# Halo rows of the plain values copied on chip instead of loaded twice, and 29 scheduling offsets in place of 12

## The chip, the cores and the metric

The kernel runs on one core of a Trainium2 chip. A core has TensorE (PE: matmuls and transposes), VectorE (DVE), ScalarE (ACT), GpSimd (POOL) and SyncE (SP), each with its own queue of instructions in a fixed order, and 16 DMA engines that all queues share. The metric is device microseconds (us) of one execution; lower is better.

## The reference

Eight batches of attention over 576 tokens and 8 heads of 64 columns, followed by an MLP over all 4,608 tokens:

```python
mask_plain = (rel >= 0) & (rel < window)                              # window 32, heads 0 to 3
mask_dil = (rel >= 0) & (rel < window * dilation) & (rel % dilation == 0)   # dilation 4, heads 4 to 7
attn = softmax(where(mask, q @ k.T / 8, -1e9));  x = attn @ v        # x: [4608, 512]
h = x @ w_in                                                          # [512, 2048]
out = (h * sigmoid(beta * h)) @ w_out
```

A plain head looks back 31 tokens. A dilated head looks back at 32 tokens of its own residue class modulo 4.

## The kernel before

**Attention of a batch b.** Plain heads are cut into six blocks of 96 queries, each against 128 keys: its own 96 and the 32 ahead of them. So the plain values lie in SBUF in a tile vp of 128 rows per block: rows 32 to 127 hold the block's own 96 value rows, rows 0 to 31 (the halo, WIN = 32) the last 32 rows of the block before. There are two such tiles, for even and odd batches. Before the change, direct_vp (L414 to L421) fetches all 128 rows of each block from DRAM, so a quarter of the rows is fetched a second time; batch 0 has three loads (96 rows of the first two heads, their 32 halo rows, and the other two heads), every later batch one. Dilated heads work on 128 of the 144 tokens of each class (scores L659, values L764), and on the last 16 of each class together, the "tail" (scores T at L628, values U at L749). Queries and keys are needed with the 64 columns on the partitions: batches 0 to 2 load rows into staging tiles st and transpose them on TensorE (dilated L461, plain L468), with copies from PSUM into kT, qT, dk, dq; from these, VectorE or GpSimd make the tail's dkt (mixed, L555) and qt, in two halves (padded, L564). Batches 3 to 7 cast q and k into DRAM scratch on GpSimd's queue and transpose by DMA on SyncE's. Scores are followed by exp on ScalarE (L595) and, from batch 1 on, a multiplication by a 0/1 mask on VectorE or GpSimd (L599); values by a normalisation on VectorE (L614, L615); the result comes into xT through transposes on TensorE (batches 0 and 1) or through DRAM by DMA.

**MLP.** Nine token tiles t of 512 tokens: 16 slices fb of four matmuls each from xT (L863), tanh on ScalarE (L872), the gate into g on VectorE (L877), then four output blocks tb in four parts of four matmuls (L898) and an eviction by 0.5 (L913, L915).

**Order.** The work is written as some 1,300 operations, each with candidate engines and an estimated duration, dependencies, a due time vt and, for some, a PSUM bank group with a cap on how many may be held (CAPS). Plan.run, a list scheduler that runs when the program is built, places one operation after another on the engine where it can start first, and among operations that can start at about the same time it takes the one with the least vt. So the order of every queue is fixed at build time, and an engine waits for its next instruction even when a later one could run. NUDGE maps the number of an operation to an offset in ns that is added to its possible start when the operations are compared. The operations are numbered as they are created, so a new operation shifts the numbers behind it. Where TensorE would be free for over 300 ns early on, the scheduler puts a "filler" matmul on zeros (L1010).

**Loads.** GpSimd issues nearly all loads, in order. For each batch below 3 (loads, from L960): dilated k and q, plain k and q, dilated values vd16, two tail pieces vt, and vp. From batch 3 on a small copy, "pace" (L976), which waits for xT (or g) of two batches before, stands ahead of a batch's casts, vd, vt and vp. A copy "spread" moves dilated values from their landing place into vd. fill3 and fill4 set the column of ones behind the values and, in fill3, zero rows of vp.

Of the kernel before, what the change touches and what calls it, by code (L numbers as in the profile page):

```python
# [36 lines left out]
class Plan:  # L37
# [3 lines left out]

    CAPS = {"h": 3, "p": 4, "o": 2, "z": 4, "a": 8, "s": 5, "w": 6}
    SWITCH = 95
    NUDGE = {101: -60, 129: 400, 159: -400, 219: 60, 245: -150, 250: 900, 417: 900, 517: 60, 554: 900,
        700: -900, 789: 60, 1116: -900}
    LAT = {"PE": 210, "ACT": 45, "DVE": 45, "POOL": 60, "SP": 0}
    NEAR = {"PE": 40, "ACT": 60, "DVE": 60, "POOL": 60, "SP": 0}

# [131 lines left out]
def kernel(  # L180
# [10 lines left out]
    nc = tc.nc  # L191
    P = 128
    B, H, S, D = q.shape
# [5 lines left out]
    WIN = 32  # L199
# [8 lines left out]
    QT = 96  # L208
    NI = S // QT
# [5 lines left out]
    DIRECT = 3  # L215
# [14 lines left out]
    plan = Plan(range(8))  # L230
# [6 lines left out]
    def copy(e, out, in_):  # L237
        (nc.scalar.copy if e == "ACT" else E[e].tensor_copy)(out=out, in_=in_)  # L238
# [46 lines left out]
    vp = [const([P, 4 * NI, DV], BF16, f"vp{i}") for i in range(2)]  # L285
# [33 lines left out]

    def t_fill3(e):  # L320
        nc.vector.memset(vp[0][:, :, D:D + 1], 1.0)
        nc.vector.memset(vp[0][0:WIN, 0, 0:D], 0.0)
        nc.vector.memset(vd[0][:, :, :, D:D + 1], 1.0)
        nc.vector.memset(vt_[0][:, :, :, D:D + 1], 1.0)
    fill3 = plan.op([("DVE", 500)], t_fill3, vt=-7.8)
# [5 lines left out]
    fill4 = plan.op([("POOL", 800)], t_fill4, vt=-1.2)  # L331
# [58 lines left out]
    def load(queue, args, deps, vt, kb, rate=.4, issue=750, lat=1100):  # L390
        return plan.op(
            [(queue, issue)],
            lambda e: dma(queue, *args), deps, vt, dma=kb * 1024 / rate / 1000, lat=lat)
# [13 lines left out]
        return [plan.op([("ACT", 175 + .834 * RD * D), ("DVE", 160 + 1.042 * RD * D)],  # L407
                        lambda e, x=x: copy(e, std[0][:, x], stage[:, x]), [o], -9.1, sbuf=True) for x in range(2)]

    def plain_v(b, p0, c0):  # L410
        return bass.AP(tensor=v.tensor, offset=v[b, 0].offset + (p0 - WIN) * D + c0 * QT * D,
                       ap=[[D, P - WIN if p0 else WIN if c0 == 1 else P], [QT * D, 4 * NI - c0], [1, D]])

    def direct_vp(b, deps, vt):  # L414
        if b:
            return [load("POOL", (vp[b % 2][:, :, 0:D], plain_v(b, 0, 0)), deps, vt, 768, .27, 1450,
                         1100 if b < DIRECT else 4000)]
        half = 2 * NI
        return [load("POOL", (vp[0][WIN:P, 0:half, 0:D], plain_v(0, WIN, 0)[:, 0:half]), deps, vt, 288, .25),
                load("POOL", (vp[0][0:WIN, 1:half, 0:D], plain_v(0, 0, 1)[:, 0:half - 1]), deps, vt, 92, .25),  # L420
                load("POOL", (vp[0][:, half:, 0:D], plain_v(0, 0, half)), deps, vt, 384, .27)]  # L421

    def direct_vd(b, deps, vt, tdeps=()):
        src = v[b, 4:8].rearrange("h (t T) d -> t h (T d)", T=C)[0:P]
# [99 lines left out]
    def attention(b, ld, names, vts):  # L524
# [3 lines left out]
        kv = b % 2  # L528
        if b < DIRECT:
            for n in [x for x in names if x[0] in "KQ"]:  # L530
                z, kind, i = "KQ".index(n[0]), n[1], int(n[2])
                vt = vt_of[n]
# [22 lines left out]
        def mixed(e):  # L555
            copy(e, dkt[kv], dk[kv][:, :, :, CT - KTL:].rearrange("p r h k -> p h k r"))
        o = plan.op([("DVE", 450), ("POOL", 550)], mixed,
                    (steps["KD0"] + steps["KD1"] if b < DIRECT else ready["D"][0:1]) + war(("dkt", kv)), vt_of["T"] - .01, sbuf=True)
# [4 lines left out]
        for c in range(2):  # L563
            def padded(e, c=c):  # L564
# [3 lines left out]
            o = plan.op([("DVE", 250), ("POOL", 500)], padded,  # L568
                        (steps["QD0"] + steps["QD1"] if b < DIRECT else ready["D"][1:]) + [fill1] + war(("qt", kv)),
                        vt_of["T"] - .01, sbuf=True)  # L570
# [5 lines left out]

        vdeps = {}
        vt = vt_of["zVAL"]
        vdeps["P", 1] = [ld["vp"][-1], (fill3, fill4)[kv]]
        vdeps["P", 0] = (ld["vp"][:-1] or ld["vp"]) + [(fill3, fill4)[kv]]  # L580
        def spread(e):
            copy(e, vd[kv][:, :, :, 0:D], vd16_of[b])
        o = plan.op([("POOL", 1100), ("DVE", 620)], spread,
                    [ld["vd"][0], (fill3, fill4)[kv]] + war(("vd", kv)), vt, sbuf=True)
# [35 lines left out]
        for name in [n for n in names if n[0] in "ST"]:  # L620
            vt = vt_of[name]
# [370 lines left out]
    for t in range(NTT):  # L992
# [4 lines left out]
        b = t + 1  # L997
# [46 lines left out]
```

## Time and profile before

| | |
|---|---|
| times of three runs | 304.8, 304.99, 305.12 us; median 304.99 |
| the profiled execution | 304.8 us; its span, first to last instruction, 303.1 us |
| PE busy | 291.2 us, 96% of the span |
| DVE, ACT, POOL busy | 188.5 (62%), 169.6 (56%), 85.6 (28%) |
| granted TensorE clock | 0.999 |
| DMA | 42.76 MB, 117,377 packets; 63.8% of the 16 engines' time on GpSimd's queue, 37.3% on SyncE's |
| issue of a vp load on GpSimd | 10 of them, 1,798 ns on average |
| landing of a vp load | 6.2 to 18.9 us after issue |

How to read it: the page gives busy time by engine, then 40 slices of the span. A busy PE is not a PE at its peak, since matmuls overlap and their ends are modelled; a matmul of 512 columns is listed with some 379 ns, but on the chain of waits four of them take 0.86 us. The chain of waits goes back from the last instruction, at each step to what released it. It is PE for 86% of the span. Idle time of an engine that nothing waits for costs nothing. Some few per cent of matmul records are missing; a gap of 0.05 us after a group of three matmuls instead of four is one of those, no stop.

By the slices the DMA engines are at 0.9 or more busy from 8 us to about 205 us, and at 0.3 or less after about 215 us; GpSimd is idle from then on.

### The profile page before, as it was taken

Reading aid. Unit: us, or ns where it says so; the run is one execution under the profiler, and the core shown is the slowest. Engines: PE = TensorE matmul, PEld = TensorE weight load, DVE = VectorE, ACT = ScalarE, POOL = GpSimd, SP = SyncE. Lnnn points to the kernel's source line nnn. Section 1 sums busy time; section 2 is a strip of 40 time slices with the busy share of each in tenths; the row PEclk is TensorE's granted clock in tenths of the full one; section 3 lists DMA queues with packets and bytes.
Section 4 is the critical chain, followed back from the end, with each engine's and each line's share of the span. In section 5 each row is a group of like instructions: output and inputs, shape, how many; then the busy total and the mean of one; then the engine's idle time right before and its main releaser. Section 6 shows DMA issues by size and latency. Waiting matters only on the chain.

```text
span 303.1 us, 5956 instructions
## 1 busy us (share of the span) xinstructions
PE 291.2 (96%) x2268; PEld 149.0 (49%) x2306; DVE 188.5 (62%) x420; ACT 169.6 (56%) x304; POOL 85.6 (28%) x123
## 2 busy tenths in 40 slices
PE   8898899899999999999999999999999999999995
PEld 5655455454544545444544444544444444444454
DVE  4768976988955966695586556956852544343300
ACT  3767764776646663765574547555743544554411
POOL 8997322853028205520560073200000000000000
PEclk9999999999999999999999999999999999999999
DMA  7999999999879998999899979995033100010122
GB/s 160 181 210 200 207 179 211 172 167 139 216 153 174 157 206 165 192 145 224 165 180 169 224 139 153 169 190 150 37 93 93 38 35 36 35 37 35 51 87 71
DMA packets 117377, 42.76 MB, mean 141 GB/s; under 512 B 93749, under 2 KB 110725, under 8 KB 117349
## 3 DMA queue, kind: packets, MB, share of 16 engines
q0 software_dynamic: 66464, 19.37, 63.8%
q1 hardware_dynamic: 50740, 22.95, 37.3%
q8 instruction: 18, 0.29, 0.4%
q14 instruction: 11, 0.08, 0.1%
q10 hardware_dynamic: 144, 0.07, 0.1%
HBM read 39.32 MB, written 18.87 MB: 192 GB/s over the span
## 4 chain that ended last, share of the span: by engine, by line
PE 86%; DMA 4%; DVE 4%; issue 3%; POOL 1%; ACT 1%; POOLq 0%; DVEq 0%
PE bank L898 41%; PE bank L863 37%; DMA st<-in_k_dram 4%; PE bank L780 2%; PE bank L659 1%; PE bank L764 1%; DVE qt L238 1%; PE bank L687 1%; PE bank L461 1%; DVE dkt L238 1%; PE bank L749 1%; PE bank L723 1%; DVE dk L238 1%; DVE g L877 0%; POOL st L388 0%
## 5 line engine op out<-in xcount | busy, mean ns | idle before, releaser
L877 DVE SCALAR_TENSOR_TENSOR g<-tnh,bank 128x512 bf16<-128x512 bf16 x144 | 97.4, 684 | 67.9 <-ACT tnh L872 66.7
L872 ACT ACTIVATE tnh<-bank,beta_half 128x512 bf16<-128x512 f32 x144 | 98.3, 690 | 73.4 <-PE bank L863 70.4
L898 PE MATMUL bank<-w_out_bf,g 128*128 128x512 bf16 (+2 forms) x589 | 137.7, 367 | 1.6 <-issue 1.1
L863 PE MATMUL bank<-xT,w_in_bf 128*128 128x512 bf16 (+1 forms) x565 | 137.2, 376 | 1.1
L863 PEld LDWEIGHTS <-w_in_bf 128*128 128x128 bf16 x584 | 55.2, 98 | 61.5 <-issue 0.4
L898 PEld LDWEIGHTS <-g 128*128 128x128 bf16 x608 | 54.7, 98 | 56.5
L913 ACT ACTIVATE osb<-bank 128x512 f32<-128x512 f32 (+1 forms) x35 | 20.6, 589 | 33.3 <-PE bank L898 32.8
L595 ACT ACTIVATE pt<-bank 128x384 bf16<-128x384 f32 (+1 forms) x54 | 20.4, 470 | 7.2 <-PE bank L687 5.3
L595 ACT ACTIVATE ptd<-bank 128x512 bf16<-128x512 f32 x32 | 16.8, 603 | 6.2 <-PE bank L659 6.2
L599 DVE TENSOR_TENSOR pt<-pt,mask_n 128x384 bf16<-128x384 bf16 (+1 forms) x43 | 15.5, 376 | 6.5 <-ACT pt L595 6.1
L615 DVE TENSOR_TENSOR xsp<-bank,rcp 96x384 bf16<-96x384 f32 x32 | 17.7, 553 | 1.1
L388 POOL DMA_DIRECT2D vp<-in_v_dram x10 | 18.0, 1798 | 0.6 <-PE bank L802 0.6
L599 DVE TENSOR_TENSOR ptd<-ptd,mask_d 128x512 bf16<-128x512 bf16 x28 | 12.2, 448 | 5.4 <-ACT ptd L595 4.5
L614 DVE RECIPROCAL rcp<-bank 128x4 f32<-128x4 f32 (+2 forms) x72 | 12.9, 179 | 4.0 <-PE bank L764 2.2
L976 POOL COPY pace<-xT 1x2 bf16<-1x2 bf16 x4 | 0.7, 176 | 50.7 <-DMA xT<-x 50.7
L615 DVE TENSOR_TENSOR xdm<-bank,rcp 128x256 bf16<-128x256 f32 x32 | 13.6, 425 | 1.1
L388 POOL DMA_DIRECT2D vt<-in_v_dram x16 | 14.2, 1030 | 0.0
L388 POOL DMA_DIRECT2D s<-in_q_dram x10 | 13.7, 1369 | 0.0
L780 PEld LDWEIGHTS <-pt 128*128 128x128 bf16 x192 | 9.1, 97 | 5.1
L388 POOL DMA_DIRECT2D s<-in_k_dram x10 | 11.2, 1122 | 1.0 <-issue 0.9
L915 DVE TENSOR_SCALAR osb<-bank 128x512 f32<-128x512 f32 (+2 forms) x3 | 1.4, 469 | 14.6 <-PE bank L898 14.6
L780 PE MATMUL bank<-vp,pt 128*128 128x65 bf16 x192 | 9.9, 193 | 0.0
(106 smaller groups left out, 172.5 us busy)
## 6 DMA issues: line engine op xcount, KB each, us to landing
out_dram<-osb SPq DMA_DIRECT2D x35, 256.0 KB, 2.8
s<-in_k_dram POOLq DMA_DIRECT2D x10, 288.0 KB, 6.3
s<-in_q_dram POOLq DMA_DIRECT2D x10, 288.0 KB, 8.5
vp<-in_v_dram POOLq DMA_DIRECT2D x7, 384.0 KB, 18.1
w_out_bf<-in_moe_w_out_dram POOLq DMA_DIRECT2D x2, 1024.0 KB, 15.2
st<-in_q_dram POOLq DMA_DIRECT2D x6, 288.0 KB, 10.8
x<-xsp SPq DMA_DIRECT2D x12, 144.0 KB
st<-in_k_dram POOLq DMA_DIRECT2D x5, 288.0 KB, 13.3
```

The lines of the kernel that those rows point to most:

```text
L238: (nc.scalar.copy if e == "ACT" else E[e].tensor_copy)(out=out, in_=in_)
L388: {"POOL": nc.gpsimd, "SP": nc.sync}[queue].dma_start(out=out, in_=in_)
L595: nc.scalar.activation(out=w(), in_=sc(), func=ACT.Exp, scale=SCALE)
L599: E[e].tensor_tensor(out=w(), in0=w(), in1=m(), op=ALU.mult)
L614: nc.vector.reciprocal(out=r, in_=p[..., D])
L615: nc.vector.tensor_tensor(out=dst, in0=p[..., 0:D], in1=r.unsqueeze(len(p.shape) - 1).to_broadcast(list(p.shape[:-1]) + [D]), op=ALU.mult)
L780: nc.tensor.matmul(pv[:, a, h2, :], lhsT=lhs, rhs=vp[kv][:, (2 * x + h2) * NI + 3 * j + a, 0:D + 1], start=True, stop=True)
L863: nc.tensor.matmul(bank(g)[:, a:z], lhsT=w_in_bf[:, kt, fb * P:(fb + 1) * P], rhs=xT[:, kt, xo + a:xo + z], start=(i == 0 and kt == kts[0] ...
L872: nc.scalar.activation(out=th[:, 0:n], in_=bank(g)[:, 0:n], func=ACT.Tanh, scale=beta_half[:, fb:fb + 1])
L877: nc.vector.scalar_tensor_tensor(out=g_t[t % 2][:, fb, c0:c0 + n], in0=th[:, 0:n], scalar=1.0, in1=bank(g)[:, 0:n], op0=ALU.add, op1=ALU.mult)
L898: nc.tensor.matmul(bank(g)[:, lo:hi], lhsT=g_t[t % 2][:, fb, tb * P:(tb + 1) * P], rhs=w_out_bf[:, fb, lo:hi], start=(fb == 0), stop=(fb = ...
L913: nc.scalar.mul(out=ob[:, lo:hi], in_=bank(g)[:, lo:hi], mul=0.5)
```

## The change

Four things are changed.

1. direct_vp loads 96 rows of each block into rows 32 to 127 of vp, all 24 blocks of a batch in one load (batch 0: two loads of 12 blocks). A new operation, halo, then copies rows 96 to 127 of each block into rows 0 to 31 of the next one of the same head, on VectorE or GpSimd: 32 partitions x 4 heads x 5 blocks x 64 columns, for batch 0 in two operations. The operations that use vp wait for the halo copy instead of the load. plain_v is gone.
2. fill3 zeroes rows 0 to 31 of the first block of all four heads, in both vp tiles, since no load writes there any more; all users of vp wait for fill3 too.
3. The estimates that the scheduler uses for a vp load become smaller: 576 KB a batch (144 a head) instead of 768, issue 1,150 ns instead of 1,450.
4. NUDGE has 29 entries instead of 12. The eight additional operations also shift the numbers.

The scheduler makes a new order of the whole program from this. Both programs have 4,613 instructions on TensorE, the same matmuls and 29 fillers; VectorE has 374 instead of 368, ScalarE 305 instead of 307, GpSimd 123 instead of 119, SyncE 103 as before. The halo copies stand on VectorE, but for batch 3's on GpSimd. What moves, early on: the plain keys of batch 1 are loaded ahead of the second weight load and transposed ahead of the first MLP matmul; the transpose of beta stands ahead of batch 0's plain transposes; in batch 1 the plain scores of one pair of heads and the tail score stand ahead of the dilated scores; in batch 2 the dilated scores stand ahead of the tail score, and batch 2's vp is loaded behind its keys instead of ahead of them. Three multiplications with the tail's mask go from VectorE to GpSimd.

```diff
--- before.py
+++ after.py
@@ -41,8 +41,10 @@
 
     CAPS = {"h": 3, "p": 4, "o": 2, "z": 4, "a": 8, "s": 5, "w": 6}
     SWITCH = 95
-    NUDGE = {101: -60, 129: 400, 159: -400, 219: 60, 245: -150, 250: 900, 417: 900, 517: 60, 554: 900,
-        700: -900, 789: 60, 1116: -900}
+    NUDGE = {75: 400, 116: -150, 160: -150, 200: -400, 206: -900, 210: 400, 221: 60, 240: -60, 250: -150,
+        280: -900, 282: 400, 298: 400, 321: -900, 332: 60, 362: -400, 373: 400, 386: 900, 395: -900,
+        408: 900, 451: -400, 454: -150, 533: 60, 539: 900, 673: 60, 822: -60, 966: -900, 976: 900,
+        1043: -900, 1066: -900}
     LAT = {"PE": 210, "ACT": 45, "DVE": 45, "POOL": 60, "SP": 0}
     NEAR = {"PE": 40, "ACT": 60, "DVE": 60, "POOL": 60, "SP": 0}
 
@@ -319,7 +321,8 @@
 
     def t_fill3(e):
         nc.vector.memset(vp[0][:, :, D:D + 1], 1.0)
-        nc.vector.memset(vp[0][0:WIN, 0, 0:D], 0.0)
+        for x in range(2):
+            nc.vector.memset(vp[x][:].rearrange("p (h i) d -> p h i d", h=4)[0:WIN, :, 0, 0:D], 0.0)
         nc.vector.memset(vd[0][:, :, :, D:D + 1], 1.0)
         nc.vector.memset(vt_[0][:, :, :, D:D + 1], 1.0)
     fill3 = plan.op([("DVE", 500)], t_fill3, vt=-7.8)
@@ -407,18 +410,21 @@
         return [plan.op([("ACT", 175 + .834 * RD * D), ("DVE", 160 + 1.042 * RD * D)],
                         lambda e, x=x: copy(e, std[0][:, x], stage[:, x]), [o], -9.1, sbuf=True) for x in range(2)]
 
-    def plain_v(b, p0, c0):
-        return bass.AP(tensor=v.tensor, offset=v[b, 0].offset + (p0 - WIN) * D + c0 * QT * D,
-                       ap=[[D, P - WIN if p0 else WIN if c0 == 1 else P], [QT * D, 4 * NI - c0], [1, D]])
-
     def direct_vp(b, deps, vt):
-        if b:
-            return [load("POOL", (vp[b % 2][:, :, 0:D], plain_v(b, 0, 0)), deps, vt, 768, .27, 1450,
-                         1100 if b < DIRECT else 4000)]
-        half = 2 * NI
-        return [load("POOL", (vp[0][WIN:P, 0:half, 0:D], plain_v(0, WIN, 0)[:, 0:half]), deps, vt, 288, .25),
-                load("POOL", (vp[0][0:WIN, 1:half, 0:D], plain_v(0, 0, 1)[:, 0:half - 1]), deps, vt, 92, .25),
-                load("POOL", (vp[0][:, half:, 0:D], plain_v(0, 0, half)), deps, vt, 384, .27)]
+
+        out = []
+        rows = vp[b % 2][:].rearrange("p (h i) d -> p h i d", h=4)
+        for hs in ((slice(0, 4),) if b else (slice(0, 2), slice(2, 4))):
+            n = hs.stop - hs.start
+            src = bass.AP(tensor=v.tensor, offset=v[b, hs.start].offset, ap=[[D, QT], [QT * D, n * NI], [1, D]])
+            o = load("POOL", (vp[b % 2][WIN:P, hs.start * NI:hs.stop * NI, 0:D], src), deps, vt, n * 144, .27,
+                     1150 if b else 750, 1100 if b < DIRECT else 4000)
+
+            def halo(e, hs=hs):
+                copy(e, rows[0:WIN, hs, 1:NI, 0:D], rows[QT:P, hs, 0:NI - 1, 0:D])
+            out.append(plan.op([("DVE", 160 + .27 * n * 320), ("POOL", 170 + 1.04 * n * 320)], halo, [o],
+                               b - 1 if b else -2.5, sbuf=True))
+        return out
 
     def direct_vd(b, deps, vt, tdeps=()):
         src = v[b, 4:8].rearrange("h (t T) d -> t h (T d)", T=C)[0:P]
@@ -576,8 +582,8 @@
 
         vdeps = {}
         vt = vt_of["zVAL"]
-        vdeps["P", 1] = [ld["vp"][-1], (fill3, fill4)[kv]]
-        vdeps["P", 0] = (ld["vp"][:-1] or ld["vp"]) + [(fill3, fill4)[kv]]
+        vdeps["P", 1] = [ld["vp"][-1], (fill3, fill4)[kv], fill3]
+        vdeps["P", 0] = [ld["vp"][0], (fill3, fill4)[kv], fill3]
         def spread(e):
             copy(e, vd[kv][:, :, :, 0:D], vd16_of[b])
         o = plan.op([("POOL", 1100), ("DVE", 620)], spread,
```

## The prediction

> **What bounds the kernel now.** I read four views: engine time in six stretches, the chain of waits from 22 to 64 us, the waits of TensorE in 20 to 64 us, and the copies into qt.
>
> Six stretches (columns: busy time and instructions of PE, PEld, DVE, ACT, POOL, then clock, DMA share, GB/s; POOL does nothing in the last):
>
> ```profile
> 0.00:20.00 20.00, 17.10 (x251) 11.58 (x252) 13.04 (x44) 11.27 (x25) 17.99 (x38) 1.00 1.22 180
> 20.00:40.00 20.00, 18.10 (x199) 10.15 (x201) 16.39 (x32) 15.11 (x30) 12.52 (x19) 1.00 1.25 205
> 40.00:64.00 24.00, 22.25 (x280) 12.63 (x282) 18.90 (x42) 14.46 (x31) 12.44 (x16) 1.00 1.62 182
> 64.00:92.00 28.00, 27.63 (x245) 14.20 (x248) 21.81 (x59) 16.83 (x35) 6.66 (x11) 1.00 1.32 170
> 92.00:212.00 120.00, 118.72 (x834) 58.36 (x849) 82.94 (x185) 71.71 (x121) 36.01 (x43) 1.00 1.39 175
> ```
>
> The clock is 1.00 throughout. PE stands idle 2.9 us before 20, 1.9 in 20 to 40, 1.75 in 40 to 64, 0.4 in 64 to 92, and 1.3 in the next 120. Both programs issue 2,306 matmuls, 29 of them fillers, so PE's work cannot change; only idle time can, and what can be won lies before 64 us.
>
> Chain of waits, 22 to 64 us (start, length, what):
>
> ```profile
> 13.71 12.40 DMA st<-in_k_dram
> 26.16 0.44 PE bank L461 x6
> ...
> 30.96 1.08 DVE qt L238
> ...
> 57.41 2.24 DVE qt L238
> 59.68 0.19 DVE qt L238
> 59.90 0.77 DVE qT L238
> ...
> 60.72 0.28 PE bank L628 x4
> ```
>
> The chain comes from batch 1's dilated keys (landed 26.11) through VectorE copies into qt; one copy takes 0.19 us, another 2.24. PE's own waits there:
>
> ```profile
> PE bank L628 <- DVE qT L238: 1.4, 1, 1.4
> PE bank L659 <- DVE g L877: 1.0, 2, 0.8
> PE bank L461 <- DMA st<-in_k_dram: 0.7, 1, 0.7
> ```
>
> The tail score of batch 2 (L628, at 60.7) waited 1.4 us for qt and qT; batch 1's dilated scores (L659, at 32.8 and 33.4) waited 1.0 for VectorE.
>
> ```profile
> L238 DVE COPY qt<-dq x11: 178/192/2243, 9.3 to 197.4; 64x128 bf16<-64x128 bf16 x11
> ```
>
> The slow copy began at 57.41; POOL's copy into vd ran from 57.93 to 59.52, and the next qt copy took 0.19 at 59.68. The 1.08 copy at 30.96 lies beside POOL's issue of a vp load (30.61 to 32.05).
>
> By the Trainium skill (SBUF — State Buffer, Who interferes with whom), a VectorE copy in a two-port mode and a GpSimd instruction exclude each other for a whole instruction; this speaks against the change, which adds eight such copies. An estimate by the rule: were each held behind POOL's longest issue, 2.52 us, VectorE would lose 20 us; by the median row above it loses nothing beyond the copies' own length.
>
> **The change, part by part.**
>
> *Smaller vp loads.* Batch 0's three (landed 12.60, 12.93, 14.12, after vd at 11.65) become two of 144 KB; the 144 KB one took 0.95 from the landing before, so the last lands at 11.65 + 2 x 0.95 = 13.55, 0.57 earlier. POOL issues them in 2 x 0.89 = 1.78 instead of 2.57: what follows on POOL moves up 0.79. A full load took 2.49 between landings around 45 us; three quarters is 1.87, 0.62 less each. Late ones took 5.2 to 6.4 between landings; a quarter less is 1.3 to 1.6. Nothing waits for them: the plain values of batch 3 are used at 93 to 103 us, and landed at 77. Gain of itself: 0.
>
> *Halo copies.* No trace row. A VectorE copy of 128x1024 into vd takes 0.43; a strided one of 128x384 0.69. Scaled to 1,280 elements: 0.5 to 2.3; I take 0.5, since vd has the same 64-element runs, and 0.3 for the two halves of batch 0. On POOL (batch 3 alone) 1.3 to 2.0, by vd's 1.04 to 1.6; nothing near follows it. These are now waits in VectorE's order: behind each stand masks and gates. Two extra memsets, 0.1 each, lie in VectorE's wait for the first keys (1.6 idle).
>
> *Start.* The beta transpose now stands ahead of the first plain transposes and dilated scores, and needs ident_f, ready at 10.22, or 9.43 after the 0.79. PE reaches it at 8.4 and stands 1.0 us; before, it stood 0.63 at about that place for dq. The exponentials start near 10.5 instead of 9.60, the values of batch 0 at 13.6 instead of 13.02. VectorE's second halo ends at 13.55 + 0.3 = 13.9, so the norms start 0.5 late, and the first MLP matmul 0.5 to 0.75 after 17.46. In these gaps now stand 36 transposes of batch 1's plain keys, 0.76 us (the group of 36 at 10.88), taken out from behind 31.0. Their load is moved ahead of two weight loads and lands at 14.12 - 0.57 + 2.59 + 1.41 = 17.55, just when needed. Net 0.
>
> *Batch 1's dilated keys* land 1.41 - 0.57 = 0.84 later, at 26.95. PE is 0.75 later too, with 0.76 of work done ahead. Net cost 0.1.
>
> *Scores of batch 1.* Plain scores of both j for one pair of heads and the tail score come first, and four MLP slices stand between the query transposes and the dilated scores. The 1.0 us wait for banks and the filler of 0.24 go. The qt copies now follow the query transposes, when POOL waits for a slot of its queue: 0.2 each.
>
> *Batch 2.* POOL's queue holds eight loads in flight (the load at 36.94 was issued when the eighth before it had landed, 36.66). With vp of batch 2 behind the keys, these land at 50.52 - 0.57 - 0.62 - 2.50 - 0.32 = 46.5, four earlier, and PE transposes them near 47.5 instead of 52.9. Query loads land 1.8 earlier, near 53.0 and 54.4; PE is there at 52.6 and 54.0: new waits of about 0.6. The dilated scores and two output slices stand ahead of the tail score, and vd's copy is on VectorE: the 1.4 us wait goes. But POOL issues batch 3's eight loads just then, beside three VectorE copies. One blocked copy costs 0 to 1.08; I take 0.6, being nearer the row at 30.96 than 0.19.
>
> *Masks.* POOL takes three tail masks (0.54 to 0.79, by its rows of 128x256 and 128x288) and three more of pt. The one at 35 us stands before vp of batch 2, which has no slot until 36.1: nothing.
>
> *Later batches.* VectorE's halo of batch 5 is ready at 137.95 (gate 14) and vp lands at 141.12 - 1.6 = 139.5: VectorE stands 1.6. PE has four slices of 0.86, the scores (0.56) and the tail score (0.13) before it needs a mask behind it, 4.1 us; VectorE needs tanh and gate 1.6, wait 1.6, halo 0.5, mask 0.45, 4.15. Hidden by a hair. Batch 7: 1.8 of wait, over 7 us of cover. Batch 4: VectorE is ready at 109.9, vp lands at 111.55 - 1.3 = 110.25; PE has three slices and 0.7 of scores, 3.3, against 1.6 + 0.4 + 0.95: hidden with 0.35 to spare.
>
> *Sum.* Ends: 1.4 + 1.0 + 0.24 idle, and 0.5 more in which the array refills after these stops (start to start they are 2.85, idle 2.35): 3.1. Comes: 0.1 + 0.6 + 0.6 = 1.3. Net 1.8 us off. The profiled run took 304.8 (span 303.1, 1.7 around it), so 303.0; the median shown is 304.99, 0.2 more: **303.2**.
>
> **Rivals.**
> - *Nothing new waits* (12%): all 3.1 go, and the other stops of 20 to 64 us too (start to start 0.33 at 44.95 and 0.83 at 25.1): 4.2 off the median, 300.8. For: PE is ahead of its loads from 38 us on. Against: VectorE is 82% busy in 20 to 40.
> - *The stalls re-form* (17%): the waits on qt went with POOL's work beside them, and that stays. Three blocked copies of 1.08 in place of one at 0.6: 0.2 off or less, about 304.8.
> - *Slower: the halo stops VectorE* (21%). Place: batches 4 and 5, just ahead of the masks. If late vp loads, sharing the engines with transposes and stores, do not land sooner for a quarter fewer rows, batch 4 waits 1.7, batch 5 3.2; less cover, PE loses 0.95 + 1.6 = 2.55: net 0.75 slower, 305.75. It decides from the point where vp lands over 22 us after its batch's first load is issued (before: 23.6 for batch 5).
> - *The doubled rows are not what costs* is no rival: bytes must fall, by 7 x 96 + 92 KB; but that may be worth nothing, as above.
>
> **How the numbers follow.** Forecast 50%, its own range 302.0 to 304.3 (new waits from 0.1 to 2.4). A measurement tells about 0.2% here, 0.6 us. Range 300.8 to 305.9. Faster is the forecast and the first rival, with a little of the second: 0.64; same: 0.15; slower: 0.21.
>
> **What would show it.** First MLP matmul near 18.1; batch 1's dilated keys landing near 26.95; no wait of PE on VectorE above 0.5 at the dilated scores of batch 1 and at the tail score of batch 2; batch 2's key transposes before 49 us; idle PE in 20 to 64 us 2.0 or less, from 3.65. Wrong if VectorE's halo has idle time of over 2 us before it and PE stands after it, or if PE waits at the query transposes of batch 2 for over 1.5.

## The result and the profile after

| | before | after |
|---|---|---|
| median (lowest to highest) | 305.06 us (304.8 to 305.33) | 306.23 us (306.05 to 306.62) |
| profiled execution, span | 304.8, 303.1 | 306.27, 304.4 |
| granted TensorE clock | 0.999 | 1.0 |
| PE busy in the span | 291.2 | 291.4 |
| DMA | 42.76 MB, 117,377 packets | 41.98 MB, 111,248 packets |

The ratio is 1.004 (95% interval 1.0023 to 1.0057): 0.4% slower, where 303.2 was forecast. Two later series of 12 runs, each beside the kernel before on another chip, gave 305.9 (1.0009, 0.9989 to 1.0028) and 305.28 (1.0016, 0.9993 to 1.004). Ratios leave out the few runs that took over 1.5% longer than the fastest of their kernel (four of 194), and are not quotients of the medians. So the loss is 0.4% in the first series and cannot be told from none in the two later ones; in these the runs of the changed kernel spread from 304.1 to 308.2, far more than a loss of that size. Why the first four lie close together, at 306.1 to 306.6, is not known.

Engine time of the changed kernel in the same stretches (columns as before):

```profile
0.00:20.00 20.00, 15.86 (x274) 11.49 (x275) 13.77 (x47) 10.69 (x23) 18.05 (x37) 1.00 1.18 176
20.00:40.00 20.00, 19.79 (x179) 11.08 (x183) 15.79 (x37) 15.79 (x30) 12.13 (x20) 1.00 1.25 206
40.00:64.00 24.00, 23.51 (x302) 13.81 (x305) 18.27 (x47) 16.98 (x35) 13.57 (x17) 1.00 1.50 179
64.00:92.00 28.00, 26.13 (x216) 13.00 (x219) 18.43 (x51) 15.64 (x33) 11.49 (x16) 1.00 1.23 158
92.00:212.00 120.00, 117.43 (x827) 57.74 (x841) 81.93 (x185) 67.89 (x116) 32.84 (x40) 1.00 1.34 173
```

TensorE's idle time is the stretch less its busy time. From 20 to 64 us it fell by 2.95, from 3.65 to 0.70. It rose by 1.24 before 20, by 1.50 in 64 to 92 and by 1.29 in 92 to 212. So up to 64 us 1.71 are gained, near the 1.8 of the forecast, and behind 64 us 2.79 are lost. Together +1.1, which is the 1.3 of the span but for 0.2. What TensorE waited for (engine and tile, releaser: us in all, times, longest):

```profile
PE bank L786 <- POOL pt L605: 1.6, 2, 1.1
PE bank L952 <- POOL ident_f masks.py:199: 1.4, 1, 1.4
...
PE bank L770 <- ACT ptt L601: 0.9, 1, 0.9
...
PE bank L770 <- DVE xdm L621: 0.3, 1, 0.3
```

The first is the plain values of batch 2, the second beta's transpose at the start, the other two the dilated values of batch 5. The chain of waits (start, length, what) names what stood behind the first and the third. The first block is taken from its window from 60 to 76 us, the second from that from 115 to 145:

```profile
61.65 11.62 DMA dq<-s
...
73.40 0.30 POOL qt L240
...
73.77 1.43 POOL pt L605 x2
```

```profile
121.94 18.19 DMA vp<-in_v_dram
...
140.22 0.48 DVE vp L240
...
140.73 0.76 DVE ptd L605 x2
```

Here are VectorE's copy and TensorE's values of batch 5 from the timelines, with the idle time before each in square brackets. The profile puts TensorE's wait down to ptt, which ended at 141.20; the mask ptd that these values need ended at 141.16, and in c_after_again and c2_after the same wait is put down to ptd.

```profile
140.22 0.48 DVE L240 COPY vp<-vp 32x1280 bf16<-32x1280 bf16 x1 [2.70 <-DMA vp<-in_v_dram]
```

```profile
141.21 0.30 PE L770 MATMUL bank<-vd,ptd 128*128 128x65 bf16 x4 [0.91 <-ACT ptt L601]
```

Two masks of batch 2 were ready for GpSimd at 71.8, when their exp was done. They stood behind a copy of batch 3's padded queries, whose transfer dq landed at 73.28. Two masks of batch 5 stood on VectorE behind the copy of the overlap rows, which waited 2.70 us for vp. In both places an engine stood at an instruction whose data was still on its way, with ready work behind it that TensorE needed. The copies into qt, whose slow one the prediction started from, are all short now:

```profile
L240 DVE COPY qt<-dq x11: 178/192/200, 9.2 to 198.7; 64x128 bf16<-64x128 bf16 x11
```

### The profile page after: what moved, and what is told of

The parts are those of the page before. It is cut to its first block, busy times and chain, and to the rows that moved or that the text cites. A ratio compares the mean times of both kernels' runs of the same rounds, so it can differ in the third digit from the quotient of the medians.

```text
span 304.4 us, 5971 instructions
## 1 busy us (share of the span) xinstructions
PE 291.4 (96%) x2269; PEld 149.7 (49%) x2306; DVE 186.1 (61%) x426; ACT 170.0 (56%) x302; POOL 88.1 (29%) x128
## 2 busy tenths in 40 slices
DMA packets 111248, 41.98 MB, mean 138 GB/s; under 512 B 87620, under 2 KB 104596, under 8 KB 111220
## 4 chain that ended last, share of the span: by engine, by line
PE 76%; DMA 12%; POOL 4%; DVE 3%; issue 3%; ACT 0%; POOLq 0%; DVEq 0%; ACTq 0%
PE bank L904 35%; PE bank L869 34%; DMA vp<-in_v_dram 6%; DMA dq<-s 4%; PE bank L786 1%; DMA xT<-x 1%; PE bank L474 1%; DMA x<-xsp 1%; PE bank L665 1%; PE bank L770 1%; PE bank L693 1%; POOL st L391 1%; PE bank L467 1%; POOL s L391 1%; DVE xdm L621 1%
## 5 line engine op out<-in xcount | busy, mean ns | idle before, releaser
L605 DVE TENSOR_TENSOR pt<-pt,mask_n 128x384 bf16<-128x384 bf16 (+1 forms) x40 | 14.1, 384 | 4.8 <-ACT pt L601 4.4
L391 POOL DMA_DIRECT2D vp<-in_v_dram x9 | 15.2, 1688 | 1.4 <-DVE pt L605 1.0
L605 DVE TENSOR_TENSOR ptd<-ptd,mask_d 128x512 bf16<-128x512 bf16 x28 | 11.0, 422 | 5.2 <-ACT ptd L601 4.5
L391 POOL DMA_DIRECT2D vt<-in_v_dram x16 | 13.3, 987 | 0.0
L786 PE MATMUL bank<-vp,pt 128*128 128x65 bf16 x192 | 10.6, 193 | 1.6 <-POOL pt L605 1.6
L921 DVE TENSOR_SCALAR osb<-bank 128x512 f32<-128x512 f32 (+2 forms) x4 | 2.1, 522 | 14.0 <-PE bank L904 14.0
```

Source lines behind the costliest of these rows:

```text
L391: {"POOL": nc.gpsimd, "SP": nc.sync}[queue].dma_start(out=out, in_=in_)
L605: E[e].tensor_tensor(out=w(), in0=w(), in1=m(), op=ALU.mult)
L786: nc.tensor.matmul(pv[:, a, h2, :], lhsT=lhs, rhs=vp[kv][:, (2 * x + h2) * NI + 3 * j + a, 0:D + 1], start=True, stop=True)
```

## The experiments

My first reading of the two traces gave three separate losses: the start (1.2), the masks of batch 2 (1.5), batch 5's overlap rows (1.2). The rival was that such waits are only the visible end of a stage that something else paces, so that removing one shows another. Each kernel below replays the changed kernel's order, written out as a list, with the named entries moved; where another order or other loads are used, that is said. Line numbers differ by a few between these kernels. Kernels of one group ran on one chip beside the kernel before. The groups, with the median of the kernel before, are e1 to e4 (305.2); c_after_again and e5 to e7 (305.04); e8 to e11 (305.14); e12 and e13 (305.3); c2_after and e14 to e16 (305.18). Times are medians with the lowest and highest run, then the ratio to the kernel before with its 95% interval.

### One wait at a time

**e1_padded_later**, GpSimd's queue:

```diff
 L240 TensorCopy dkt_129<-dk_125 128x384
-L240 TensorCopy qt_123<-dq_127 64x128
 L605 TensorTensor pt<-pt,mask_n 128x3x96 x2
-L240 TensorCopy qt_123<-dq_127 64x128
+L240 TensorCopy qt_123<-dq_127 64x128 x2
```

> The changed kernel with one GpSimd instruction moved: the copy of the padded dilated queries of batch 3 (qt<-dq, which waits for dq to land at 73.28) stands behind the two plain masks of batch 2 (pt) on GpSimd instead of ahead of them. Theory (an in-order wait on GpSimd's queue cost TensorE 1.07 + 0.48 at 73 to 75 us): both masks run near 72.3 us, the two TensorE waits at the plain values of batch 2 go, TensorE's idle time in 64 to 92 falls from 1.87 to about 0.4, the time falls by 1.2 to 1.5 to about 304.9. Rival (TensorE's wait there is only the visible end of a stage that VectorE or ScalarE paces): another wait takes its place, idle time in 64 to 92 stays above 1.3, the time stays within 0.4 of 306.2.

305.14 (304.3 to 305.84), 0.9993 (0.9983 to 1.0002). The waits at the masks are gone, as expected. The size is not fixed, though: in six profiles of kernels that keep this order of GpSimd (the changed kernel three times, e2, e3, e9) TensorE waited there 1.56, 0.88, 0, 0.21, 0 and 0 us, because dq landed at 73.3 in the first, at 72.1 in the second and at 70.9 to 71.5 in the others. The mean is 0.44.

**e2_halo5_pool**, batch 5's overlap copy:

```diff
 DVE: L883 TensorScalarPtr g_91<-tnh_94,bank_70 128x512
-DVE: L240 TensorCopy vp_131<-vp_131 32x4x5x64
 DVE: L605 TensorTensor ptd<-ptd,mask_d 128x512 x2
 ...
 POOL: L240 TensorCopy qt_123<-dq_127 64x128
+POOL: L240 TensorCopy vp_131<-vp_131 32x4x5x64
 POOL: L982 TensorCopy pace<-xT 1x2
```

> The changed kernel with batch 5's copy of the 32 overlap rows moved from VectorE's queue to the end of the same batch's work on GpSimd, which is idle there. Theory (VectorE stood 2.70 us for the landing of vp at 140.1, ahead of masks and gates that were ready): TensorE's waits of 0.91 at 141.2 and 0.32 at 142.7 go, the time falls by 0.9 to 1.3 to about 305.1; vp lands within 0.5 of 140.1 and GpSimd's copy takes about 1.25. Rival (the gates of that stage were late anyway, since VectorE has 0.1 to spare): the time falls by less than 0.4.

304.3 (303.17 to 305.63), 0.9968 (0.9953 to 0.9984). TensorE's waits at 141 and 142 are gone from the profile; vp landed at 138.44, 18.8 after its issue. Now VectorE stood 1.34 before batch 6's copy, but TensorE lost nothing by it.

**e3_beta_later**:

```diff
 PE:  L1016 Matmult bank_72<-zero 128x256
-PE:  L952 Matmult bank_71<-ident_f,beta_row 128x16
 PE:  L474 Ldweights st_115
 ...
 PE:  L718 Matmult bank_67<-add_P,ident_b 128x192
+PE:  L952 Matmult bank_72<-ident_f,beta_row 128x16
```

> The changed kernel with TensorE's transpose of beta put back behind the second set of plain masks of batch 0 (as before the change), and its scaling on VectorE behind the copy of vd. Theory (the wait of 1.37 for ident_f at 8.5 to 9.9 is what put the start late): the plain key transposes begin near 8.8 instead of 10.0, the first dilated scores near 9.5 instead of 10.7, VectorE's first norm near 14.1 instead of 15.3, first matmul of the MLP near 18.8 instead of 19.9, the time falls by 0.9 to 1.2 to about 305.2. Rival (the two overlap copies on VectorE, which wait for vp to land at 12.5 and 13.4, hold the norms by themselves): the first norm at 14.8 or later, the time falls by less than 0.6.

305.58 (303.85 to 309.38), 1.0014 (0.9995 to 1.0034). The theory failed: no gain that can be told. The wait of 1.37 went and the first norm came at 14.1, but TensorE then stood 0.80 for the plain keys of batch 1 at 18.3, and the first full MLP matmul came at 19.57 instead of 19.91.

**e4_three**, these three edits together:

> The changed kernel with the three moves together (padded queries of batch 3 behind the masks of batch 2 on GpSimd; batch 5's overlap rows on GpSimd; beta's transpose late). Theory (three separate in-order waits, each lost in full): the falls add up to 3.0 to 3.9, the time is 302.4 to 303.2, below both kernels. Rival (slack is shared, a stall removed early comes back at the next landing): less than two thirds of the sum of the three single falls.

304.74 (302.74 to 306.0), 0.9972 (0.9953 to 0.9991). Its profiled run, 305.12, had the granted clock at 0.92 in 10 to 20 us and 0.91 in 20 to 30, and a stop of 0.92 behind the overlap copy of batch 6, whose vp landed 18.5 us after issue instead of 15.7. So batch 5's is not the only place for such a stop, and the sum could not be read from this kernel. The record has more of this: before batch 6's copy VectorE stood 0.03 in the five profiles in which batch 5's copy, too, is on VectorE (the changed kernel three times, e1, e3), and 1.34, 2.47 and 1.18 in those in which it is on GpSimd (e2, e4, e15). In part the rival holds: the wait that is taken away at batch 5 can come back at batch 6. The line of the changed kernel, then that of e15:

```profile
168.05 0.48 DVE L240 COPY vp<-vp 32x1280 bf16<-32x1280 bf16 x1
```

```profile
167.65 0.48 DVE L240 COPY vp<-vp 32x1280 bf16<-32x1280 bf16 x1 [1.18 <-DMA vp<-in_v_dram]
```

### Which place counts

**c_after_again** is the changed kernel, no edit.

> The changed kernel itself once more, beside the others on the same chip. Theory (its order puts short instructions behind transfers whose landing differs by 1 to 3 us from one execution to the next: dq of batch 3 landed at 73.3, 71.1, 71.4, 70.9 and 74.6 in the five profiles of this order so far): median 305.7 to 306.3, and its runs spread over more than 1.5 us, where the kernel before keeps within 1.2. Rival (its 1.2 us over the kernel before are a fixed stall of the order): every run within 0.4 of 306.2.

305.9 (304.14 to 308.87), 1.0009 (0.9989 to 1.0028). The median and the spread agree with the theory.

**e5_halos_pool** moves the overlap copies of batches 4, 5, 6 and 7 as e2 moves batch 5's, and the padded queries as e1:

> The changed kernel with the overlap rows of batches 4, 5, 6 and 7 copied by GpSimd, last of their batch in its queue, and the padded queries of batch 3 behind the masks of batch 2 on GpSimd. Nothing of this order then stands on VectorE behind a late load of values. Theory: TensorE has no wait over 0.3 us between 64 and 212 us in the profile; the median is 303.6 to 304.3 and the spread is below that of the changed kernel. Rival (GpSimd's copies of 1.25 us disturb VectorE's copies, or the stalls move on): median above 304.7.

302.81 (302.5 to 303.51), 0.9917 (0.9893 to 0.9942): 0.8% below the kernel before, on the chip where the changed kernel took 305.9, and lower than either theory had it. Its idle time from 64 to 212 is back at that of the kernel before (0.32 and 1.33):

```profile
64.00:92.00 28.00, 27.68 (x226) 13.81 (x228) 19.84 (x53) 17.54 (x35) 11.16 (x16) 1.00 1.28 175
92.00:212.00 120.00, 118.67 (x835) 58.35 (x849) 82.40 (x182) 69.17 (x117) 38.20 (x45) 1.00 1.36 169
```

GpSimd's copy of 1.25 us costs nothing there, as the timeline of its queue shows (start, length, instruction, idle before):

```profile
138.24 1.25 POOL L240 COPY vp<-vp 32x1280 bf16<-32x1280 bf16 x1 [5.39 <-DMA vp<-in_v_dram]
141.89 0.17 POOL L982 COPY pace<-xT 1x2 bf16<-1x2 bf16 x1 [2.40 <-DMA xT<-x]
```

**e9_halos_alone** has e5's overlap copies without the move of the padded queries:

> The changed kernel with the overlap rows of batches 4 to 7 on GpSimd, and nothing else moved: the padded queries of batch 3 stay ahead of the masks of batch 2. Together with that move as well the time was 302.81. Theory (the copies that wait on VectorE are the greater part of the loss): 303.0 to 303.8, with 0.3 to 1.0 of TensorE's waits at the masks near 73 us still in the profile. Rival (the masks of batch 2 are the greater part): above 304.3.

304.03 (302.68 to 307.35), 0.9955 (0.994 to 0.9971): between the theory's and the rival's range. In its profile dq landed early and TensorE did not wait at the masks.

To share the loss out on one chip, four kernels ran together: **c2_after** (the changed kernel), **e14_all_but_b5** (e5 with batch 5's copy back on VectorE), **e15_b5_and_masks** (e5 with those of 4, 6 and 7 back) and **e16_best_again** (e5).

> The changed kernel beside the next three on one chip, so that the parts of its loss are measured against each other there. Expected by both theories: 305.5 to 306.3, spread over 1.5.

> The changed kernel with the padded queries of batch 3 behind the masks of batch 2 and the overlap rows of batches 4, 6 and 7 on GpSimd; batch 5's stay on VectorE. Theory (batch 5's copy alone holds TensorE, 0.9 to 2.1 us by the profiles, batches 4, 6 and 7 land before they are needed): 304.3 to 305.0. Rival (the others stand as often, as batch 6 did once for 0.9): 303.2 to 303.9.

> The changed kernel with the padded queries of batch 3 behind the masks of batch 2, and only batch 5's overlap rows on GpSimd. Theory (batch 5 alone): within 0.5 of the next run, 302.8 to 303.4. Rival (batches 4, 6, 7 as well): 1 or more above the next run.

> The changed kernel with the padded queries of batch 3 behind the masks of batch 2 and the overlap rows of batches 4 to 7 on GpSimd, the same kernel that gave 302.81, on the chip of the three runs before this one. Expected by both theories: 302.5 to 303.3, 2.5 to 3.3 below the changed kernel.

| | median | ratio, interval |
|---|---|---|
| c2_after | 305.28 (304.08 to 308.19) | 1.0016 (0.9993 to 1.004) |
| e14_all_but_b5 | 305.23 (303.9 to 308.0) | 1.0003 (0.9984 to 1.0023) |
| e15_b5_and_masks | 304.47 (302.94 to 305.51) | 0.9976 (0.9959 to 0.9993) |
| e16_best_again | 303.59 (302.5 to 304.03) | 0.9948 (0.993 to 0.9966) |

Moving batch 5's copy as the last one (e14 to e16) is worth 1.64 us, and the intervals do not touch. Without it the other moves bring nothing that can be told (c2_after to e14). Batch 5's copy and the masks without those of 4, 6 and 7 (c2_after to e15) bring 0.8, with intervals that touch. All together are worth 1.7 here, not the 2.5 to 3.3 that were expected, and 3.1 on the chip of e5. So batch 5's copy is the one whose place counts; whether its full price shows only where the later copies, too, have left VectorE, these intervals do not settle. The step from e15 to e16, 0.9, is not settled: its intervals overlap, and e15's profiled run lost 0.88 at 101 us behind a VectorE copy into vd that waited for its load, and 0.79 at 57.9, neither of them an overlap copy. Its wait of VectorE before batch 6's copy, 1.18, cost TensorE nothing in that profile. e14's profiled run, 308.0, shows the place at its worst, VectorE first, then TensorE (its granted clock dipped just behind this wait, which adds to its time; see the last section):

```profile
140.18 0.48 DVE L240 COPY vp<-vp 32x1280 bf16<-32x1280 bf16 x1 [3.96 <-DMA vp<-in_v_dram]
140.70 0.76 DVE L605 TENSOR_TENSOR ptd<-ptd,mask_d 128x512 bf16<-128x512 bf16 x2
```

```profile
138.72 0.28 PE L634 MATMUL bank<-qt,dkt 128*128 128x64 bf16 x4
141.18 0.30 PE L770 MATMUL bank<-vd,ptd 128*128 128x65 bf16 x4 [2.18 <-DVE ptd L605]
```

In the six profiles with batch 5's copy on VectorE (changed kernel three times, e1, e3, e14) TensorE lost 1.24, 1.31, 1.13, 1.27, 2.22 and 2.18 there, mean 1.56, close to the 1.64 of the runs.

### The start

**e6_start_before** is e5 with batch 0's three loads of doubled rows, no overlap copies for it, and the order of TensorE, VectorE and ScalarE of the kernel before up to the seventh gate of the first MLP tile; GpSimd keeps the new order.

> The kernel of the run before this one, with the start as it was: batch 0's plain values by three loads with doubled rows and no overlap copies, and the order of TensorE, VectorE and ScalarE up to the seventh gate of the first MLP tile as before the change (beta's transpose late, dilated scores first, the plain key transposes of batch 1 after the MLP has begun). Theory (the start lost 1.2 to 1.5 and nothing in it was won): first matmul of the MLP near 17.5 instead of 19.9, with 0.76 less done ahead, and the median 1.2 to 1.7 below the run before this one, about 302.4. Rival (TensorE, earlier, meets the landing of the dilated keys of batch 1 at 27.1 and stands there for as long): less than 0.5 below it.

304.1 (303.51 to 305.07), 0.9958 (0.994 to 0.9976): 1.3 above e5. The rival holds, and more than that: the new start is the better one. The first MLP matmul came at 17.52 instead of 19.70, but what was won was lost at the next landing:

```profile
PE bank L470 <- DMA st<-in_k_dram: 1.1, 1, 1.1
PE bank L907 <- DVE g L886: 0.8, 1, 0.8
...
PE bank L758 <- DVE dk L240: 0.4, 1, 0.4
```

The first is batch 1's dilated keys, landed at 27.48, the third the copy behind them, the second the gates behind a held copy of vd (last section); idle time in 20 to 40 was 1.85, as before the change, against 0.21 in e5.

**e11_beta_later** is e5 with e3's edit.

> The best order so far (302.81) with beta's transpose put back behind the plain masks of batch 0, so that TensorE no longer waits 1.37 for ident_f at 8 to 10 us. Theory (the start is not on the path, since the MLP's first tile meets the keys of batch 1 that land at 18 and 27 us whatever the start does): within 0.4 of 302.8, with a TensorE wait on st<-in_k_dram of 0.7 to 1.3 near 17 to 18 us in place of the one on ident_f. Rival (the start's 1.2 is lost in full): 301.8 or less.

302.66 (302.34 to 304.18), 0.9926 (0.9904 to 0.9949): the same ratio as e5's on another chip, as far as can be told, with waits of 0.31 for the keys at 17.6 and again at 26.8 in place of the one for ident_f. So my first reading of the start was wrong: the 1.24 us of idle time ahead of 20 us are not a loss that an earlier start wins back.

### The loads themselves

**e7_loads_only** keeps the order of the kernel before; batches 1 to 7 are loaded without doubled rows, with an overlap copy on VectorE for batch 1 and on GpSimd for the others, there just ahead of "pace" and the issues of the next batch.

> The kernel before, its order kept, with the plain values of batches 1 to 7 loaded without doubled rows and the 32 overlap rows copied by VectorE (batch 1, ahead of its plain masks) and GpSimd (2 to 7, last of their batch in its queue). Theory (the smaller load by itself buys nothing: vp lands no sooner, and the issue of 0.3 us less on GpSimd is not on the path): within 0.3 of the kernel before, 304.9 to 305.5. Rival 1 (a quarter fewer rows brings the landing forward by over 1 us, and with it the loads that are queued around it): 0.5 or more faster. Rival 2 (GpSimd's copies slow VectorE): 0.5 or more slower.

307.28 (305.72 to 308.93), 1.0065 (1.0039 to 1.0091). The size is that of the second rival, the way is one that it did not name: GpSimd's copy at 54.70 put its issues 1.1 later, and VectorE's copies beside them took longer. VectorE, then TensorE:

```profile
57.07 3.67 DVE L240 COPY qt<-dq 64x128 bf16<-64x128 bf16 x2
```

```profile
61.59 0.28 PE L637 MATMUL bank<-qt,dkt 128*128 128x64 bf16 x4 [2.58 <-DVE qT L240]
```

Before the change the same two copies took 2.47 and the wait was 1.38. These 1.2 are not the whole of the loss: in six of the twelve runs the granted clock dipped as well (last section), and their median is 308.19; that of the other six is 306.11, 1.1 above the kernel before.

**e8_loads_only_b2** is e7 with batch 2's copy on VectorE at about 51 us:

> As the run of the smaller loads in the old order, but with batch 2's overlap rows copied by VectorE in its idle time near 51 to 53 us, so that GpSimd issues the next batch's loads as early as in the kernel before. In that earlier run GpSimd's copy put these issues 1.1 later, VectorE's two short query copies at 57.1 then took 3.67 instead of 2.47 and TensorE waited 2.59 instead of 1.38 for qT. Theory (that was the cost): the two copies take about 2.5 again, TensorE's wait at 58.6 is 1.4 again, and the time is within 0.4 of the kernel before, 304.7 to 305.5. Rival (the smaller loads themselves are in the way somewhere): 0.8 or more slower than the kernel before.

304.78 (304.44 to 305.09), 0.9986 (0.9976 to 0.9996): the copies took 2.34, the wait was 1.25, and the loads alone are worth 0.4 us (0.1 to 0.7 by the interval).

**e10_doubled_rows** is e5 with doubled rows and no overlap copies for batches 1 to 7 (the source of the load; its destination becomes all 128 rows):

```diff
-            src = bass.AP(tensor=v.tensor, offset=v[b, hs.start].offset, ap=[[D, QT], [QT * D, n * NI], [1, D]])
+            src = bass.AP(tensor=v.tensor, offset=v[b, hs.start].offset - (WIN * D if b else 0),
+                          ap=[[D, P if b else QT], [QT * D, n * NI], [1, D]])
```

> The best order so far (302.81), but with the plain values of batches 1 to 7 loaded with doubled rows as before the change and no overlap copies for them; batch 0 as changed. Theory (the gain is in the order, none of it in the smaller loads): 302.3 to 303.3; vp lands as long after its issue as without doubled rows (14 to 18.5 us), GpSimd's issue takes 2.5 instead of 2.2. Rival (a quarter fewer rows relieves the queues): 303.8 or more.

303.67 (302.98 to 304.82), 0.9952 (0.9935 to 0.9969): 0.9 above e5 on another chip and 1.0 above e11 on the same one, with intervals that overlap. TensorE stood where the prediction had feared it, at batch 2's query loads:

```profile
53.70 0.69 PE L469 MATMUL bank<-ident_b,st 96*128 96x96 bf16 x12 [0.32 <-DMA st<-in_q_dram]
...
55.63 0.47 PE L476 MATMUL bank<-ident_b,st 64*64 64x64 bf16 x18 [0.38 <-DMA st<-in_q_dram]
```

**e12_vd_scalar** is e11 with batch 2's copy of vd moved from VectorE (55.9 us) to ScalarE (60.0), and **e13_vd_scalar_doubled** is e12 with doubled rows.

> The kernel of the run before this one (overlap rows of batches 4 to 7 on GpSimd, padded queries behind the masks, beta's transpose late: 302.66, runs from 302.34 to 304.18), with batch 2's copy of the dilated values (vd) moved from VectorE at 55.9 us to ScalarE, into its idle time near 59.5. In five profiles in which that copy began 0.25 to 0.36 us after GpSimd's long issue of s<-in_k_dram it took 1.74 to 1.85 us and ended 0.43 after the issue's end, and TensorE then waited 0.77 to 0.78 for the gates behind it; where it began 0.12 to 0.13 after, it took 0.42. Theory (VectorE's copy is held by that issue): TensorE's wait near 57.7 is gone from the profile, the median falls to 301.9 to 302.4 and the spread to less than 1 us. Rival (the wait is only the visible end of another limit in that stage): TensorE still waits 0.5 or more between 55 and 62, median 302.6 or more.

> The kernel of the run before this one, with the plain values of batches 1 to 7 loaded with doubled rows and no overlap copies for them, on the same chip. Theory (the smaller loads are worth something only between 25 and 64 us, where the queues are full: with doubled rows the query loads of batch 2 land 0.5 to 1 us later and TensorE waits some 0.7 for them near 53 to 55): 0.5 to 0.9 slower than the run before this one. Rival (they are worth nothing in any order): within 0.3 of it.

e12: 303.7 (302.57 to 305.03), 0.9955 (0.9938 to 0.9972). The wait near 57.7 is gone, but the time did not fall: a miss. Its profiled run lost time to the granted clock, as told in the last section, but that is not the whole of it: its six runs without such a dip have a median of 303.49, hardly below the 303.59 of e16 on the same chip. The rest stays open. e13: 305.14 (304.28 to 305.87), 0.9994 (0.9985 to 1.0003), 1.4 above e12 on the same chip, with intervals apart. So in this order the smaller loads, with their overlap copies, are worth 1.4 us, more than either theory gave them. In e13's profile one landing of xT came late enough for a wait of 1.1 at 143 us.

## Why the prediction was wrong

The sum was right on the two waits that the profile had shown. It was wrong where it scaled a landing, and where it booked nothing for the masks.

| step of the prediction | forecast | measured |
|---|---|---|
| waits at batch 1's dilated scores and batch 2's tail score go | idle 20 to 64 at most 2.0 | 0.70; neither wait is left |
| batch 1's dilated keys land | 26.95 | 27.11 |
| batch 2's key transposes | near 47.5 | 47.85 |
| query loads of batch 2: new wait | 0.6 | 0 (0.70 with doubled rows, e10) |
| one blocked VectorE copy | 0.6 | 0 in this profile; 0.77 to 0.79 in seven others |
| first MLP matmul | near 18.1 | 19.91 |
| start | net 0 | idle time before 20 us 1.24 more, but no loss in the runs (e11, e6) |
| masks on GpSimd | nothing | 1.56 here, 0.44 in the mean of six |
| smaller loads of themselves | 0 | a gain of 0.4 (e8) to 1.4 (e13) |
| batch 5's overlap copy | "Hidden by a hair" | 1.24 here, 1.56 in the mean of six |

**The step that failed** is "vp lands at 141.12 - 1.6 = 139.5" under the later batches. A quarter fewer rows was taken for a quarter less time between landings. The load landed 18.2 us after its issue, as before (18.25), and 23.7 after its batch's first load, beyond the point of 22 that the third rival named; and VectorE stood 2.70 before the copy with TensorE standing after it, which the prediction itself gave as a sign of being wrong. With that landing the prediction's own balance, cover 4.1 against 1.6 + wait + 0.5 + 0.45, gives a loss of 1.15 for the 2.70 that VectorE stood; TensorE lost 0.91 + 0.32. So the mechanism of the rival "the halo stops VectorE" was right for batch 5, and its price there, 1.6, met the mean of six. It was not right for batch 4, which cost TensorE 0.1 at most in these profiles, and it had nothing of the masks; that its 305.75 lies near the 305.9 of a later series is in part luck. It should have had more than a chance of 21%, since the row that spoke for it, 14.6 to 18.9 us from issue to landing among late loads of one size, was in the trace. And "Hidden by a hair" does not follow from the prediction's own sum, where VectorE needs 4.15 against a cover of 4.1: even with the early landing nothing was to spare.

The second miss, "Masks: nothing", counted the time of the moved instructions and looked at one of six in its queue. Two pt masks had been put behind a copy that waits for a DMA. The third, the start, came out at net 0 by a way that was not the one worked out: TensorE began the MLP 1.8 us later than forecast, and the landings of batch 1's keys at 18 and 27 us took up that delay. So the near hit up to 64 us, 1.71 for 1.8, is one of the total and not of its terms: the two new waits of 0.6 did not come in this profile, and the start had 1.24 more idle time than before.

One sum among the rivals is wrong. For *The stalls re-form*, three copies of 1.08 in place of one at 0.6 cost 2.6 more; that turns 1.8 off into some 0.8 slower, near 305.8, and not into 304.8.

With the late overlap copies and the masks out of the way (e5, e16) the forecast's 303.2 stands between the two series of that kernel, 302.81 and 303.59. The gain was real; two in-order waits took it back. One of them was foreseen as a rival and is shown by e14 against e16; that of the masks is shown by the profiles, but in the runs its removal alone brings nothing that can be told.

## What to carry to other kernels

A copy that replaces part of a load turns a landing that nobody waited for into a wait in an engine's queue: price it with the landing as it was, and with its spread over the batches, and put it last in the queue of an engine that is idle there. Before a delay is booked as a loss, look for the next landing that TensorE meets anyway; before one is booked as covered, ask for a margin larger than the spread of the landing it rests on. When an order is made anew, look, for each instruction that waits for a DMA, at the ready work that stands behind it.

## What the runs showed of the hardware

**Landings spread.** In kernels with one and the same order of loads, dq of batch 3 took 9.7 to 11.8 us from issue to landing, vp of batch 5 17.1 to 19.7 and vp of batch 6 15.6 to 18.9. Not all of this is chance: batch 6's took 15.6 to 17.0 with batch 5's overlap copy on VectorE (six profiles) and 17.8 to 18.9 with it on GpSimd (eight). In one and the same kernel dq took 9.7, 10.6 and 11.6 (the changed kernel), and vp of batch 4 16.4 and 19.6 (e5 and e16). A quarter fewer rows did not shorten vp's (18.2 and 14.6 before, for batches 5 and 6).

**A VectorE copy beside GpSimd's issue of a DMA can be held until the issue is over.** Batch 2's vd copy (128x1024) took 0.42 to 0.43 where it began 0.12 to 0.24 us after the start of GpSimd's issue of s<-in_k_dram, whose own time then grew from 1.67 to between 1.68 and 1.81 (seven profiles). Where it began 0.25 to 0.36 after, in seven profiles, it took 1.74 to 1.85 and ended 0.43 after the issue did; where it began 1.29 after (e10), it took 0.81 and ended 0.43 after the issue. e5 (VectorE) and e11 (VectorE, then GpSimd, then TensorE behind the gates):

```profile
55.58 0.42 DVE L240 COPY vd<-vd 128x1024 bf16<-128x1024 bf16 x1
```

```profile
55.87 1.77 DVE L240 COPY vd<-vd 128x1024 bf16<-128x1024 bf16 x1
```

```profile
55.55 1.67 POOL L391 DMA_DIRECT2D s<-in_k_dram  x1
```

```profile
58.89 1.02 PE L904 MATMUL bank<-w_out_bf,g 128*128 128x512 bf16 x4 [0.77 <-DVE g L883]
```

The Trainium skill (SBUF — State Buffer, Who interferes with whom) says that whoever issues first holds the shared ports for a whole instruction and the other is fully blocked. The rows agree that the one that loses waits for the whole of the other; which of the two counts as first they do not settle, since by the recorded starts the issue came first each time. The overlap copies, on which the prediction weighed that rule, were not held where they are whole: the six on VectorE took 0.48 each for 1,280 elements. The second half of batch 0's, which began at 14.65 beside an issue of a vt load (14.57), took 0.76 in the changed kernel, where the same copy took 0.30 in e16.

**The granted clock can dip to half for 3.4 us.** In 29 of the 190 runs of these kernels that the comparisons use the mean clock was 0.993 or 0.994, in 2 of 137 of the kernel before. In each of the six profiled runs of that kind the dip is a single stretch of 3.4 us at 0.50. It began at 11.4 us in c_after_again, at 17.8 to 18.4 in e4, e12 and e13, at 62.2 in e7 and at 141.9 in e14. The window of e7's (columns as before), and the page of e12 with a digit per 7.5 us, where it lies in the third slice:

```profile
62.17:65.58 3.41, 3.41 (x23) 1.45 (x21) 1.57 (x4) 1.43 (x4) 2.58 (x2) 0.50 1.84 165
```

```profile
PEclk9979999999999999999999999999999999999999
```

In e12, 18 transposes then took 0.69 instead of the 0.47 of e11, and the first MLP matmuls came at 19.78 instead of 19.08. In five of the six TensorE had stood in the last 0.8 us before the dip or stood as it began, for 2.58 us (e7), 2.18 (e14), 1.30 (e4), 0.62 (e13) and 0.33 (e12). Whether such a wait brings it on was not tried; waits of 1.38 (before the change) and 1.90 (e3) went by without one. It is neither a matter of the start nor of the new order alone: e7, which keeps the order of the kernel before, had it in six of twelve runs.
